# Moving three pieces of a fused attention and two-layer kernel: y products one tile earlier, the first units' stores to GpSimd's queue, and two pieces of the last product to an earlier pool

## The chip, the cores and the metric

The kernel runs on one core of a Trainium2 chip. The metric is device time in microseconds of one execution; each kernel is run several times and the median is given. TensorE (PE, with its weight loads PEld), VectorE (DVE), ScalarE (ACT), GpSimd (POOL) and SyncE (SP, which only issues DMAs here) each run their own instructions in the order in which they stand in the program.

## What is computed

The reference, cut to what matters:

```python
def _attn_ref(q, k, v):                      # (8, 8, 576, 64), chunks of 64
    scores = scale * q_c @ k_c.T
    attn = softmax(scores)
    return attn @ v_c
def _moe_ref(x, w_in, w_out, g_ln):          # 4608 tokens, 512 -> 1024 -> 512
    h = x @ w_in
    solu = h * softmax(h)
    ln = (solu - mean) / sqrt(var + 1e-06) * g_ln
    return ln @ w_out                        # "y" below
def _moe2_ref(x, w_in, w_out, alpha):        # 512 -> 2048 -> 512
    h = x @ w_in
    g = maximum(h, 0) + alpha * minimum(h, 0)
    return g @ w_out
reference = moe2(moe(attention(q, k, v)))
```

Every matrix product is made to float32 accuracy out of three products of a high and a low part (high by high, high by low, low by high).

## The kernel before, in words

**Phase 1** walks over 36 tiles of 128 tokens: attention, `h`, softmax and layer norm, transposed back (`zt`, `zh`, `zl`), then the y product of the tile. Its order is written out by hand: `FIRST` for the first ten tiles, then `STEP` (line 70) once for every tile i from 10 to 35, then `LAST` (line 81). An entry such as `ye-7` does the step `ye` of tile i-7; an entry that has been done already is passed over. `LAST` begins with `zh34 zl34 ya30 yb30 ye29 zt35 zh35 zl35 ye30 ya31`. `ya` and `yb` (`ymm`, line 567) are the two halves of one y product, `ye` (`yevac`, line 582) copies it out of PSUM on ScalarE and stores it. A y product s needs the tiles of its pair (s and s+1 for even s). The PSUM tile `yps` has one buffer; for `LAST` a second one is opened (line 654), and product s takes the one with number (s+1) mod 2. The `zh`/`zl` pairs have three buffers (line 177), the PSUM tile `zt` has one (line 182).

**Phase 2, first product.** The 4608 tokens are six groups s of 768 (each as two halves of 384 columns), the 2048 columns of the layer eight blocks b. Strassen's scheme makes a unit (`unit`, line 821) out of seven products `p1 p6 p5 p7 p2 p3 p4` in the PSUM tiles x, y, z, v, and four results `g` of it: "22", "11", "12", "21", in this order, in six buffers. Each is stored by a DMA `gd<-g` on SP (`store`, line 806). The results "12" and "21" are finished and stored inside the next unit (`late`, line 809). `load_y` (line 721) fetches the next group's y, `sum_y` (line 729) adds its parts on GpSimd; both are called from `extra` (line 1003), at places named (b, k). In the first group the weights of blocks 4 to 7 are also loaded by `extra`.

**Phase 2, second product.** It is cut into 40 pieces x = (chunk c, group g, block pair j), the first of them (0,0,0) to (0,0,3). A piece is loaded (`load_g`, line 897: a, b, c and, from the results "11", "12", "22", "21"), turned into operands (`prepare`, line 918: on DVE three operations for p1, three for p5, one each for p6 and p7, with copies on ScalarE) and multiplied (`multiply`, line 940). Piece (0,0,0) is loaded and prepared beside the last group's units, in the slots that group's y leaves free (`slot`, line 712: a list of 25), and its `t4` lies in a pool of its own (line 690). The others lie in the pool `rp` (line 1036), which is opened after the pool of these slots has been closed and takes over its memory: a load into it waits until what lay there has been read. SP takes eight DMAs in flight: each waits for the one eight places ahead of it on the DMA queues of SP and ScalarE.

Of the kernel before, what the change touches and what calls it, by code (L numbers as in the profile page):

```python
# [33 lines left out]
SG = 384  # L34
# [8 lines left out]
def order(text):  # L43
# [25 lines left out]
)  # L69
STEP = order(  # L70
    """
    q+3 v+3 ye-7 zh-2 zl-2 conv+0 hm+0 tr+1 te+1 qk+2 hx+0 he+0 qm+2 qe+2 pv+1 zt-1 xn+1 so+0 sq+0
    ya-6 conv+1 xt+1 xh+1 xl+1 zv+0 pw+0 qs+2 zs+0 yb-6
    """
)
CONV = order(
# [13 lines left out]
def tile_chunk_attention_solu_prelu(  # L90
# [30 lines left out]
    wo_dram = dram.tile([128, NB2, 2, 7, 256], F32, name="wod")  # L121

    g_dram = [dram.tile([128, NB2, PAIRS], F32, name=f"gd{i}") for i in range(4)]

    def fetch64(raw, src):

# [555 lines left out]
    def phase2():  # L682
        with ExitStack() as c2:
            def P(name, bufs, side="left", stack=c2, **k):
                return stack.enter_context(tc.tile_pool(name=name, bufs=bufs, side=side, reuse_waits="tile", **k))
# [1 line left out]
            NL = 2  # L687
            wl = P("w2l", 1)
            ps2 = [P("ps_2l", 1, space=PSUM)]
            kp = P("k4", 1)  # L690
            ca = c2.enter_context(ExitStack())
            tp = P("t2", 1, stack=ca)
            up = P("u2", 1, stack=ca)
# [12 lines left out]

            slots = [f"y{i}" for i in range(25)]
            homes = {}  # L710

            def slot(dtype, name):
# [36 lines left out]
            class Unit:  # L749
# [54 lines left out]
                    )  # L804

                def store(self, t):
                    nc.sync.dma_start(out=GD[t][:, self.b, self.s * SG:self.s * SG + SG], in_=self.g[t])

                def late(self, k):

# [76 lines left out]

            def new(x, tag, dtype=F32R):
                n = CHUNKS[x[0]][1]
                if x == (0, 0, 0):  # L890
                    if tag == "t4":
                        return kp.tile([128, 2, n], dtype, name="t4", tag="t4")
                    return slot(dtype, f"f{tag}")[:, :, :n]
                bufs = dict(t3=1, t2=1, t4=4, hi=4, lo=3).get(tag, 2)
                return rp.tile([128, 2, 512], dtype, name=f"r{tag}", tag=tag, bufs=bufs)[:, :, :n]

            def load_g(x):
                c, g, j = x
                p0, n = CHUNKS[c]
                for tag, t in (("a", "11"), ("b", "12"), ("c", "22"), ("d", "21"))[2 * g:]:  # L900
                    src[x, tag] = new(x, tag, F32 if tag == "b" else F32R)
                    nc.sync.dma_start(
                        out=src[x, tag].bitcast(F32), in_=GD[t][:, 2 * j:2 * j + 2, p0:p0 + n]
                    )

            def split(x, p, f, out):
                h = new(x, "hi")
# [10 lines left out]
            def prepare(x, p):  # L918
                a, b, c, d = (src.get((x, t)) for t in "abcd")
                k = x[0], x[2]  # L920
                if p == "p1":
                    low_ = split(x, p, a, a)
                    t3 = src[x, "t3"] = new(x, "t3", F32)
                    dsub(t3, c, b)
                    dsub(b, b, a)
                    low_()
                elif p == "p5":
                    low_ = split(x, p, b, None)
                    t2 = src[x, "t2"] = new(x, "t2", F32)
                    dsub(t2, c, b)  # L930
                    t4 = t4s[k] = new(x, "t4", F32)
                    dsub(t4, d, t2)
                    low_()
                else:
                    f = dict(p6=src.get((x, "t2")), p7=src.get((x, "t3")), p2=d, p3=c, p4=t4s.get(k))[p]
                    split(x, p, f, f if p in ("p2", "p3") else None)()

            bank, acc, out_ = {}, {}, []

# [61 lines left out]
            for s in range(NS):  # L1001
                for b in range(NB2):
                    def extra(k):
                        if s == 0 and k == 1 and NL + 2 + b < NB2:
                            load_w(NL + 2 + b, wi_dram)
                        if s + 1 == NS:
                            x = (0, 0, 0)
                            if (b, k) == (0, 3):
                                load_g(x)
                            if k == 2 and 4 <= b:  # L1010
                                prepare(x, GROUPS[0][b - 4])
                        else:
                            if (b, k) == (0, 3):
                                load_y(s + 1)
                            if (b, k) in sums:
                                sum_y(sums[b, k])
                            if (b, k) in early:
                                high_y(s + 1, early[b, k])
                            if (b, k - 1) in early:
                                low_y(s + 1, early[b, k - 1])  # L1020
# [8 lines left out]
                        load_w(b, wo_dram)  # L1029
            for k in range(3):  # L1030
                prev.late(k)
            for t in range(4):
                multiply(t)
            ca.close()

            rp = P("g3", 2)
            op = P("o3", 1)
            LEAD = 3
            load_g(pieces[1])
            load_w(6, wo_dram)  # L1040
            load_g(pieces[2])
            load_w(7, wo_dram)
            for t in range(4, 4 + LEAD):
                prepare(steps[t][:3], steps[t][3])
            for t in range(4, len(steps)):
                for n, x in enumerate(pieces[3:], 3):
                    if start[pieces[n - 2]] + 2 == t:
                        load_g(x)
                if t + LEAD < len(steps):
                    prepare(steps[t + LEAD][:3], steps[t + LEAD][3])  # L1050
                multiply(t)
                evacuate(t)
# [36 lines left out]
```

## Time and profile before

| | |
|---|---|
| median of 3 runs | 1329.59 us (1328.49 to 1331.25) |
| the profiled execution | 1325.93 us |
| its span in the profile | 1324.1 us |
| PE busy | 1266.7 us, 96% |
| DVE, ACT, POOL busy | 946.5, 689.6, 328.9 us |
| granted clock, mean | 0.987 |

The profile is one execution; times in it count from the start of its span. Phase 1 ends and phase 2 begins at about 599 us, the second product begins at about 967 us. A busy PE says that matmuls were in it, and the granted clock (PEclk, 1.00 is full speed) how fast they could go.

### The profile page before, as it was taken

To read this page: it belongs to the slowest core of one execution; us is meant where nothing else is said; L and a number is where in the kernel's file an instruction comes from. 1 tells how busy PE (TensorE), PEld (TensorE's weight loads), DVE (VectorE), ACT (ScalarE), POOL (GpSimd) and SP (SyncE) were. 2 spreads that over 40 slices of the span, in tenths; PEclk is the share of its full clock that TensorE was granted. 3 is DMA by queue.
4 is the path that set the end of the run, shared out by engine and by line. 5 is a ranking of instruction groups with operands and counts; after the bars stand their busy time and mean duration, and the time that the engine had idled before them with its cause. 6 is when DMAs were issued, how large, how long until landed. Compare 5 with 4: busy or idle time off the path is not lost. (4 is left out here: it accounts for less than half of the span.)

```text
span 1324.1 us, 21433 instructions
## 1 busy us (share of the span) xinstructions
PE 1266.7 (96%) x7968; PEld 1167.5 (88%) x7968; DVE 946.5 (71%) x1425; ACT 689.6 (52%) x1140; POOL 328.9 (25%) x309
## 2 busy tenths in 40 slices
PE   4989989999999999998999999999989999999998
PEld 3778879999899989997999999999989888888898
DVE  6996676777767677424777777777766968868584
ACT  4685455555655654433656666666544444444443
POOL 4664254444645554222020202110000000000000
PEclk9799999999999999999999999999989999999999
DMA  9774267565757563348542433436985827465462
GB/s 232 173 169 117 82 164 176 147 172 167 216 163 215 169 190 128 106 170 340 207 156 102 161 123 136 149 114 234 323 313 156 281 85 272 140 232 197 135 231 96
DMA packets 214792, 236.30 MB, mean 178 GB/s; under 512 B 89248, under 2 KB 174240, under 8 KB 212640
## 3 DMA queue, kind: packets, MB, share of 16 engines
q1 hardware_dynamic: 204896, 225.49, 54.4%
q10 hardware_dynamic: 9792, 9.44, 2.1%
q8 instruction: 63, 1.03, 0.3%
q14 instruction: 41, 0.34, 0.1%
HBM read 148.90 MB, written 85.98 MB: 177 GB/s over the span
## 5 line engine op out<-in xcount | busy, mean ns | idle before, releaser
L802 DVE SCALAR_TENSOR_TENSOR g<-ng,nal,g 128x384 f32<-128x384 f32 x192 | 123.3, 642 | 62.2 <-ACT g L680 62.2
L160 PE MATMUL yps<-zh,wo_h 128*128 128x256 f32 x576 | 167.2, 290 | 0.0
L162 PE MATMUL yps<-zh,wo_l 128*128 128x256 f32 x576 | 163.0, 283 | 0.0
L161 PE MATMUL yps<-zl,wo_h 128*128 128x256 f32 x576 | 162.8, 283 | 0.0
L680 ACT ACTIVATE ng<-g 128x384 f32<-128x384 f32 x144 | 75.7, 526 | 140.4 <-DVE g L674 140.4
L763 PE MATMUL hx<-th,w 128*128 128x384 f32 x384 | 113.8, 337 | 5.0 <-ACT s L680 5.0
L763 PE MATMUL hv<-th,w 128*128 128x384 f32 x384 | 114.1, 337 | 4.2 <-DVE g L674 3.9
L763 PE MATMUL hz<-th,w 128*128 128x384 f32 x384 | 114.0, 337 | 2.9 <-DVE wv L674 2.9
L161 PEld LDWEIGHTS yps<-zl,wo_h 128*128 128x128 f32 x576 | 110.4, 192 | 0.1
L160 PEld LDWEIGHTS yps<-zh,wo_h 128*128 128x128 f32 x576 | 110.4, 192 | 0.1
L162 PEld LDWEIGHTS yps<-zh,wo_l 128*128 128x128 f32 x576 | 110.2, 191 | 0.0
L950 PE MATMUL oz<-rhi,w 128*128 128x512 f32 (+1 forms) x312 | 96.7, 371 | 1.2 <-DVE osb L674 1.2
L950 PE MATMUL ox<-rhi,w 128*128 128x512 f32 (+1 forms) x312 | 97.2, 373 | 0.0
L950 PE MATMUL ov<-rhi,w 128*128 128x512 f32 (+1 forms) x312 | 95.9, 368 | 0.0
L677 POOL TENSOR_TENSOR yt<-y,y 128x384 f32<-128x384 f32 x24 | 29.1, 1232 | 246.3 <-DMA y<-yd 197.2
L680 ACT ACTIVATE rhi<-rt 128x1024 fp32r<-128x1024 f32 (+1 forms) x57 | 55.5, 982 | 61.2 <-DVE rt L677 18.4
L481 PE MATMUL h<-wi_h,xh 128*128 128x512 f32 x256 | 71.0, 399 | 7.8 <-ACT xh L467 5.2
L763 PEld LDWEIGHTS hv<-th,w 128*128 128x128 f32 x384 | 71.3, 189 | 6.6 <-DVE g L674 4.9
L680 ACT ACTIVATE g<-g 128x384 f32<-128x384 f32 x144 | 75.2, 522 | 3.1
L763 PEld LDWEIGHTS hx<-th,w 128*128 128x128 f32 x384 | 71.3, 189 | 5.3 <-ACT s L680 5.3
L561 DVE TENSOR_TENSOR zl<-zt,zh 128x1024 fp32r<-128x1024 f32 x36 | 44.0, 1222 | 44.0 <-ACT zh L556 44.0
L763 PEld LDWEIGHTS hz<-th,w 128*128 128x128 f32 x384 | 71.3, 189 | 4.3 <-ACT th L680 4.3
(188 smaller groups left out, 3340.8 us busy)
## 6 DMA issues: line engine op xcount, KB each, us to landing
gd<-g SPq DMA_DIRECT2D x192, 192.0 KB, 1.9
w<-wid SPq DMA_DIRECT2D x8, 1792.0 KB, 10.6
w<-wod SPq DMA_DIRECT2D x8, 1792.0 KB, 9.7
rc<-gd SPq DMA_DIRECT2D x24, 512.0 KB, 4.0
rd<-gd SPq DMA_DIRECT2D x24, 512.0 KB, 4.9
raw<-in_moe_w_out SPq DMA_DIRECT2D x24, 511.8 KB, 4.2
qt<-in_q SPq DMA_DIRECT2D x36, 256.0 KB, 5.1
kbd<-in_k SPq DMA_DIRECT2D x72, 128.0 KB, 5.1
```

Of the source, the lines that this page charges most:

```text
L160: nc.tensor.matmul(o, lh, rh, start=first, stop=False)
L161: nc.tensor.matmul(o, lh, rl, start=False, stop=False)
L162: nc.tensor.matmul(o, ll, rh, start=False, stop=last)
L481: nc.tensor.matmul(ps[:, n], xh[:, kk], w[:, kk, 512 * n:512 * n + 512], start=(kk == 0 and w is wi_h), stop=False,)
L561: nc.vector.tensor_tensor(out=zl, in0=ps, in1=zh.bitcast(F32), op=ALU.subtract)
L677: eng.tensor_tensor(out=out, in0=a, in1=b, op=ALU.subtract)
L680: nc.scalar.activation(out=out, in_=in_, func=func, **k)
L763: nc.tensor.matmul(self.ps[x], w[:, a, i, k], d[:, k], start=(p not in CHAINED and k + j == 0), stop=(k == 1 and j == 2), skip_group_check ...
L802: nc.vector.scalar_tensor_tensor(out=self.g[t], in0=self.n[t], scalar=nal_sb[:, f:f + 1], in1=self.g[t], op0=ALU.mult, op1=ALU.add)
L950: nc.tensor.matmul(bank[key, m][:, :n], W[2 * j + k][:, a, i, 128 * m:128 * m + 128], d[:, k], start=(p not in CHAINED and j + k + q == 0) ...
```

## The change

The y products stand one tile nearer in `STEP`. In the first group all 32 stores of `g` go to GpSimd's DMA queue. Pieces (0,0,0) and (0,0,1) both lie in the y slots (one more of these, no `k4` pool); a slot is given back as soon as its last reader has been recorded; their `t4` is written to DRAM by GpSimd and read back for the second half of the chunk. Piece (0,0,1) is loaded at place (7,1) of the last group, prepared after its last unit and multiplied next. The last step of piece (0,0,0) is prepared at (7,0) rather than (7,2). The pieces after it are loaded one later, and weights 6 ahead of piece (0,0,2).

```diff
-    q+3 v+3 ye-7 zh-2 zl-2 conv+0 hm+0 tr+1 te+1 qk+2 hx+0 he+0 qm+2 qe+2 pv+1 zt-1 xn+1 so+0 sq+0
-    ya-6 conv+1 xt+1 xh+1 xl+1 zv+0 pw+0 qs+2 zs+0 yb-6
+    q+3 v+3 ye-6 zh-2 zl-2 conv+0 hm+0 tr+1 te+1 qk+2 hx+0 he+0 qm+2 qe+2 pv+1 zt-1 xn+1 so+0 sq+0
+    ya-5 conv+1 xt+1 xh+1 xl+1 zv+0 pw+0 qs+2 zs+0 yb-5
...
+    t4_dram = [dram.tile([128, 2, CHUNKS[0][1]], F32, name=f"t4d{i}") for i in range(2)]
...
-            kp = P("k4", 1)
-            slots = [f"y{i}" for i in range(25)]
+            slots = [f"y{i}" for i in range(26)]
...
                 def store(self, t):
-                    nc.sync.dma_start(out=GD[t][:, self.b, self.s * SG:self.s * SG + SG], in_=self.g[t])
+                    eng = nc.gpsimd if self.s == 0 else nc.sync
+                    eng.dma_start(out=GD[t][:, self.b, self.s * SG:self.s * SG + SG], in_=self.g[t])
...
             def new(x, tag, dtype=F32R):
-                if x == (0, 0, 0):
-                    if tag == "t4":
-                        return kp.tile([128, 2, n], dtype, name="t4", tag="t4")
-                    return slot(dtype, f"f{tag}")[:, :, :n]
+                if x in pieces[:2]:
+                    return slot(dtype, f"f{tag}")
...
             def load_g(x):
+                if x in ((0, 1, 0), (0, 1, 1)):
+                    t4s[0, j] = new(x, "t4", F32)
+                    nc.sync.dma_start(out=t4s[0, j], in_=t4_dram[j])
...
             def prepare(x, p):
+                done = free if x in pieces[:2] else lambda t: None
                 if p == "p5":
...
+                    for t in (b, c, d):
+                        done(t)
+                    if x in pieces[:2]:
+                        nc.gpsimd.dma_start(out=t4_dram[x[2]], in_=t4)
+                        done(t4)
                 else:
...
+                    if p in ("p6", "p7"):
+                        done(f)
...
-                            x = (0, 0, 0)
                             if (b, k) == (0, 3):
-                                load_g(x)
-                            if k == 2 and 4 <= b:
-                                prepare(x, GROUPS[0][b - 4])
+                                load_g(pieces[0])
+                            if (b, k) == (7, 1):
+                                load_g(pieces[1])
+                            if (b, k) in ((4, 2), (5, 2), (6, 2), (7, 0)):
+                                prepare(pieces[0], GROUPS[0][b - 4])
...
-            for t in range(4):
+            load_w(6, wo_dram)
+            for p in GROUPS[0]:
+                prepare(pieces[1], p)
+            for t in range(8):
                 multiply(t)
             ca.close()
...
-            load_g(pieces[1])
-            load_w(6, wo_dram)
             load_g(pieces[2])
             load_w(7, wo_dram)
-            for t in range(4, 4 + LEAD):
+            load_g(pieces[3])
+            for t in range(8, 8 + LEAD):
                 prepare(steps[t][:3], steps[t][3])
-            for t in range(4, len(steps)):
-                for n, x in enumerate(pieces[3:], 3):
+            for t in range(8, len(steps)):
+                for n, x in enumerate(pieces[4:], 4):
```

**GpSimd at the start of phase 2** (`gd<-g` is a store of a result, `yt<-y` and `y<-y` are the sums of the next group's y). Before:

```order
L873 TENSOR_SCALAR nal<-al_sb 128x16
L677 TENSOR_TENSOR yt_6846<-y_6793,y_6791 128x384 x2
L677 TENSOR_TENSOR y_6791<-y_6791,y_6789 128x384 x2
L677 TENSOR_TENSOR yt_7013<-y_6793,y_6791 128x384 x2
L677 TENSOR_TENSOR yt_7097<-y_6795,yt_7013 128x384 x2
```

and with the change:

```order
L875 TENSOR_SCALAR nal<-al_sb 128x16
L809 DMA gd_76<-g 128x384
L809 DMA gd_73<-g 128x384
L679 TENSOR_TENSOR yt_6845<-y_6792,y_6790 128x384 x2
L809 DMA gd_74<-g 128x384
L809 DMA gd_75<-g 128x384
L809 DMA gd_76<-g 128x384
L809 DMA gd_73<-g 128x384
L679 TENSOR_TENSOR y_6790<-y_6790,y_6788 128x384 x2
L809 DMA gd_74<-g 128x384
L809 DMA gd_75<-g 128x384
```

The first two stores ("22" and "11" of the first unit) stand ahead of the first sum; "12" and "21" of the first unit and "22" and "11" of the second stand behind it.

**ScalarE at the end of phase 1** (`zh<-zt` are the copies of tiles 33 to 35, `ysb<-yps` the copies of y products). Before:

```order
L556 ACTIVATE zh<-zt 128x8x128
L586 ACTIVATE ysb<-yps 128x512
L588 DMA yd_69<-ysb 128x2x256
L556 ACTIVATE zh<-zt 128x8x128
L586 ACTIVATE ysb<-yps 128x512
L588 DMA yd_70<-ysb 128x2x256
L586 ACTIVATE ysb<-yps 128x512
```

and with the change:

```order
L558 ACTIVATE zh<-zt 128x8x128
L238 ACTIVATE hi<-s_6130 128x512
L238 ACTIVATE hi<-s_6131 128x512
L503 ACTIVATE eh,st<-h,st 128x1024
L519 ACTIVATE eh,st<-sl,st 128x1024
L558 ACTIVATE zh<-zt 128x8x128 x2
L588 ACTIVATE ysb<-yps 128x512
L590 DMA yd_70<-ysb 128x2x256
L588 ACTIVATE ysb<-yps 128x512
```

The y product 29 has been copied out inside `STEP`, and the copies of tiles 34 and 35 now follow each other; the first copy behind them is that of y product 30.

**SP at the end of the last group**, with the engines that each DMA waits for (`gd<-g` are the last unit's stores, `w<-wod` weights 6 and 7, `fa` to `fd` the piece in the y slots, `ra` to `rd` pieces in the pool `rp`). Before:

```order
L807 DMA gd_76<-g 128x384 [waits DMAHW0_49,DVE_49]
L807 DMA gd_73<-g 128x384 [waits DMAHW1_49,DVE_49]
L807 DMA gd_74<-g 128x384 [waits DMAHW2_49,DVE_49]
L807 DMA gd_75<-g 128x384 [waits DMAHW3_49,DVE_49]
L902 DMA ra<-gd_73 128x2x384 [waits DMAHW4_49,PE_49]
L902 DMA rb<-gd_74 128x2x384 [waits PE_49,DMAHW5_49,Activation_49,Pool_49]
L902 DMA rc<-gd_76 128x2x384 [waits DMAHW6_49,PE_49,Activation_49]
L902 DMA rd<-gd_75 128x2x384 [waits DMAHW7_49,PE_49]
L705 DMA w_10883<-wod 128x3584 [waits DMAHW0_49]
L902 DMA ra<-gd_73 128x2x384 [waits DMAHW1_49]
L902 DMA rb<-gd_74 128x2x384 [waits DMAHW2_49]
L902 DMA rc<-gd_76 128x2x384 [waits DMAHW3_49]
```

and with the change:

```order
L902 DMA fc<-gd_76 128x2x384 [waits DMAHW2_49,DMASW4_49,Activation_49]
L902 DMA fd<-gd_75 128x2x384 [waits DMASW7_49,DMAHW3_49,DMASW3_49,PE_49]
L809 DMA gd_76<-g 128x384 [waits DMAHW4_49,DVE_49]
L809 DMA gd_73<-g 128x384 [waits DMAHW5_49,DVE_49]
L809 DMA gd_74<-g 128x384 [waits DMAHW6_49,DVE_49]
L809 DMA gd_75<-g 128x384 [waits DMAHW7_49,DVE_49]
L706 DMA w_10818<-wod 128x3584 [waits DMAHW0_49]
L902 DMA ra<-gd_73 128x2x384 [waits DMASW5_49,DMASW1_49,DMAHW1_49,DVE_49,PE_49]
L902 DMA rb<-gd_74 128x2x384 [waits DMASW6_49,DMASW2_49,DMAHW2_49,PE_49,Pool_49]
L902 DMA rc<-gd_76 128x2x384 [waits DMAHW3_49,DMASW4_49]
L902 DMA rd<-gd_75 128x2x384 [waits DMAHW4_49,DMASW7_49,DMASW3_49]
L706 DMA w_10964<-wod 128x3584 [waits DMAHW5_49]
```

The piece behind the one in the slots is now loaded ahead of the last unit's stores, into slots (`fa` to `fd`), and the first `ra` to `rd` are the third piece's; weights 6 stand ahead of them. The second of these four loads, `rb`, has a wait for PE. By the count in the built program this is the last matmul with the low part of p6 of the piece before, (0,0,1), the third of its four products.

## Rows read from the trace of the kernel before

**Rows 1.** The page, busy time of each engine

```profile
PE 1266.7 (96%) x7968; PEld 1167.5 (88%) x7968; DVE 946.5 (71%) x1425; ACT 689.6 (52%) x1140; POOL 328.9 (25%) x309
```

**Rows 2.** Windows: length, busy PE, PEld, DVE, ACT, POOL (count); PEclk; DMA; GB/s

```profile
180.00:190.00 10.00, 4.78 (x23) 3.96 (x23) 7.94 (x16) 6.25 (x11) 2.52 (x4) 0.84 0.84 190
...
620.00:630.00 10.00, 5.11 (x16) 5.11 (x17) 6.42 (x11) 4.43 (x10) 7.83 (x8) 0.68 1.05 397
...
980.00:990.00 10.00, 10.00 (x44) 10.00 (x45) 7.94 (x10) 3.27 (x4) 0.00 (x0) 0.73 1.01 396
```

**Rows 3.** Timeline, PE, h of tile 11: start, us, line, count [idle before <-releaser]

```profile
186.91 2.08 PE L481 MATMUL h<-wi_h,xh 128*128 128x512 f32 x4 [5.22 <-ACT xh L467]
188.79 1.71 PE L481 MATMUL h<-wi_l,xh 128*128 128x512 f32 x4
190.33 1.08 PE L481 MATMUL h<-wi_h,xh 128*128 128x512 f32 x4
```

**Rows 4.** Windows, the matmuls of y alone, two products (29 and 30)

```profile
558.10:569.90 11.80, 11.75 (x96) 11.58 (x96) 0.60 (x1) 1.00 1.01 374
```

**Rows 5.** Timelines of PE, DVE and ACT, end of phase 1

```profile
569.75 1.04 PE L543 MATMUL zt<-ident,sl 128*128 128x128 f32 x8
...
564.11 1.50 DVE L532 TENSOR_SCALAR sl<-sl,st 128x1024 f32<-128x1024 f32 x1 [0.66 <-POOL st L528]
565.53 1.21 DVE L561 TENSOR_TENSOR zl<-zt,zh 128x1024 fp32r<-128x1024 f32 x1
...
570.82 1.03 ACT L556 ACTIVATE zh<-zt 128x1024 fp32r<-128x1024 f32 x1 [5.12 <-PE zt L543]
571.74 0.60 ACT L586 ACTIVATE ysb<-yps 128x512 f32<-128x512 f32 x1
```

**Rows 6.** Timelines of PE, DVE and POOL, start of phase 2

```profile
624.89 0.69 PE L763 MATMUL hx<-th,w 128*128 128x384 f32 x1 [5.02 <-ACT s L680]
...
621.91 0.56 DVE L674 TENSOR_TENSOR g<-hz,u 128x384 f32<-128x384 f32 x1 [5.80 <-DMA gd<-g]
...
626.55 0.56 DVE L674 TENSOR_TENSOR g<-hv,wv 128x384 f32<-128x384 f32 x1
...
619.17 1.96 POOL L677 TENSOR_TENSOR yt<-y,y 128x384 f32<-128x384 f32 x2 [46.62 <-DMA y<-yd]
```

**Rows 7.** DMA issues: count, KB, us to landing; the last at 600.25

```profile
gd<-g SPq DMA_DIRECT2D x192, 192.0 KB, 1.9
...
yd<-ysb ACTq DMA_DIRECT2D x36, 256.0 KB, 2.1
...
yd<-ysb ACTq DMA_DIRECT2D x1, 256.0 KB, 13.4
```

**Rows 8.** Chain that ended last: start, us, what (first, third piece)

```profile
967.23 2.08 PE ox L950 x12
...
990.75 2.08 PE ox L950 x12
```

**Rows 9.** Timelines of PE and DVE, start of the second piece

```profile
979.74 0.69 PE L950 MATMUL ox<-ra,w 128*128 128x384 f32 x1 [3.85 <-DVE ra L677]
...
976.67 0.96 DVE L677 TENSOR_TENSOR rt<-rc,rb 128x768 f32<-128x768 f32 x1 [6.23 <-DMA rc<-gd]
```

**Rows 10.** Timelines of ACT and DVE in the last unit

```profile
962.84 0.84 ACT L680 ACTIVATE fhi<-ft 128x768 fp32r<-128x768 f32 x1
...
962.56 0.56 DVE L674 TENSOR_TENSOR u<-hy,s 128x384 f32<-128x384 f32 x1 [0.20 <-ACT s L680]
...
963.56 0.55 DVE L674 TENSOR_TENSOR wv<-hz,u 128x384 f32<-128x384 f32 x1
964.03 0.95 DVE L677 TENSOR_TENSOR flo<-ft,fhi 128x768 fp32r<-128x768 f32 x1
```

**Rows 11.** DMA issues from 969.9 to 972.6: count, KB, us to landing

```profile
ra<-gd SPq DMA_DIRECT2D x1, 384.0 KB, 3.6
rb<-gd SPq DMA_DIRECT2D x1, 384.0 KB, 4.1
```

## The prediction

> **What bounds the kernel now.** I read the busy times first: TensorE has matmuls in it for 96% of the span [rows 1], so only its idle time can be won, and time in which its clock is low. The windows show where that is: three stretches of ten us have little work or a granted clock of 0.84, 0.68 and 0.73 [rows 2]. 1.00 is the 2.4 GHz level; a mean below it mixes 2.4 and 1.2 GHz. The change touches all three, so I went to the timeline of each. In the first, TensorE idles 5.22 before the h product of tile 11, for which ScalarE's copy is late; the product then starts slowly, 2.08 and 1.71 for four matmuls that take 1.08 at full speed, so 1.6 is lost [rows 3]. In the second, at the start of phase 2, VectorE waits 5.80 for a store of `g` to land, and TensorE 5.02 [rows 6]. In the third, TensorE idles 3.85 before the second piece of the last product, whose load VectorE waited 6.23 for [rows 9]. Each time the clock fell behind idle time of 3.85 or more. The cost of a fall is 1.6 (counted matmul by matmul), 2.7 and 3.2 (27% and 32% of ten us, a little of it in idle time) [rows 2, 3]. I use these three as the price of a fall.
>
> **The y products.** Two y products take 11.75, one 5.9 [rows 4]. *At the beginning*: step 10 had no y product, because its entry was done already. Now it has one, in the place where TensorE idled. The h product of tile 11 starts at 181.7 + 5.9 = 187.6 instead of 186.9, at full speed: -1.6 + 0.7 = -0.9. From there each step holds the next y product in the same place, and its inputs are two tiles old or more, so nothing changes until the end. *At the end*: one y product less stands between the last h product and the transpose of tile 35, so TensorE reaches that at 569.75 - 5.9 = 563.9. But the transpose's PSUM tile is free only when VectorE has made the low part of tile 34, which stands behind the scaling of tile 35 and ends at 565.53 + 1.21 = 566.7 [rows 5]. This chain hangs on the last h product and doesn't move: TensorE idles 2.9. Then y product 31 has to use the PSUM tile of product 30 (now made while there was only one), and the copy that frees it stands behind tile 35's on ScalarE. In these rows that copy ends 571.74 + 0.60 - 569.75 = 2.6 after the transpose began, so there are 1.6 more idle behind a transpose of 1.0 [rows 5]. Against a product of 5.9 stand 4.5 idle: -1.4. Together -2.3. The idle 2.9 and 1.6 have only a transpose between them, and I expect the clock to fall there: its price is 1.6 to 3.2, I take 2.4. **Sum of this part: +0.1, ends -2.3 and +0.9.**
>
> **The stores.** Today the first unit's stores stand on SP behind weights and y. In GpSimd's queue the first two ("22", "11") can go at once, and the second unit's wait of 5.80 goes. What is late next: "12" and "21" stand behind the first `sum_y`, and GpSimd waits in that until the y loads have landed; it begins at 619.17 and takes 1.96 [rows 6]. VectorE needs the buffer of "12" for the third unit's first result. Queued behind the waiting GpSimd are these two stores and the second unit's; VectorE, then TensorE, wait for them. So "12" goes at 621.1, when weights 5 to 7 fill the DMA engines: 3 x 1792 KB, at the 397 GB/s of that stretch [rows 2] some 14 us, until about 634. No row shows a store of GpSimd's queue. The low end is a store as on the page, 1.9 [rows 7]: landed at 623.0, and the third unit's first result comes 3.5 before today's 626.55 [rows 6]. The high end is the one store that another queue made beside such loads: ScalarE's of y took 13.4 instead of 2.1 [rows 7]. It has two rows of 1 KB per partition, a `g` store has one; half of the extra 11.3 makes 5.6, so 7.5 to landing and 5.6 for each one behind it. Then "12" lands at 628.6, 2.1 later than today's result, and the third store behind the sums at about 636, where today's third result of that unit is 3 behind its first, at 629.5. Of these 6.5 late the next unit's first products, on the other PSUM tiles, cover about 2: +4.5. The first row is of an idle moment and the second of ScalarE's queue; neither is nearer, so I take the middle: **+0.5, ends -3.5 and +4.5.** TensorE idles some 4 or more there either way, so the clock falls as it does today and its price is in both.
>
> The Trainium skill (DMA: Bandwidth & Descriptors, section Issuing engines are not separate DMA queues) speaks against this part: DMAs of all issuing engines run on the same 16 DMA engines and interleave, and another issuing engine only saves the time to issue. The row of ScalarE's store, 13.4 beside the loads, agrees with it; by that rule the sum would be nearer the high end.
>
> GpSimd's own time for 32 stores, and for two stores of `t4`, lies beside an engine that is 25% busy [rows 1]; were it over 1.5 a store it would hold up the next sums, which have three units of slack. The two `t4` stores and loads are 384 KB each, against some 3.6 for such a load alone [rows 11], and are due tens of us later: nothing.
>
> **The pieces.** Piece (0,0,1) is loaded before the last unit's stores and is multiplied right behind the first: the idle 3.85 goes. Against this stand two things. *The last step of piece (0,0,0)* is prepared earlier in the last unit, and VectorE then waits in it for ScalarE's copy `fhi`, which ends at 962.84 + 0.84 = 963.7; with its 0.95 behind that, `u` starts at 964.6 instead of 962.56, and `wv` ends at 966.1 instead of 964.1 [rows 10]. Product p3 needs that; it began two products of 1.04 before the first piece, at 965.1 [rows 8]. So the first piece starts 1.0 later, at 968.2. *The third piece's load*: the load of b waits for p6 of the second piece, because its memory held that operand, and c stands behind b. Eight products of 2.08 [rows 8] end at 984.9, the third of the second piece's four at 982.8. b is issued then and c half a us later; first and second of a row of loads take 3.6 and 4.1 [rows 11], so c lands at 987.4. From VectorE's first operation on it to TensorE's start there are 979.74 - 976.67 = 3.1 [rows 9]: the third piece starts at 990.5. It starts at 990.75 now [rows 8]. So the stall isn't removed but moved by one piece, to 5.6 of idle time, and -0.2 is left. The slow stretch behind today's stall is inside the 990.75; the new one comes after the 990.5. It costs again 1.6 to 3.2, I take 2.7, the row of the stall it replaces. **+2.5, ends +1.4 and +3.0.** Weights 6 and 7 and the fourth piece land some 8 us ahead of their use; the work behind is the same.
>
> **Sum:** 0.1 + 0.5 + 2.5 = +3.1. The profiled execution took 1325.93, so 1329.0 for such a one; the median of the runs is 1329.59, 3.7 above it, and with the same difference I get 1332.7. The ends together make -4.4 and +8.4.
>
> **Rivals.**
> *GpSimd's queue is slow* (the high end): the third and fourth unit wait for stores behind the sum. For it: the 13.4 row, and a GpSimd that waits to 621. Against: the store has half the rows. 0.1 + 4.5 + 2.5 = +7.1: 1336.7. This is also the case in which that part doesn't do what it says.
> *GpSimd's queue is quick*: its stores land in about 1.9 beside the loads. 0.1 - 3.5 + 2.5 = -0.9: 1328.7. The Trainium skill (the same page, section Queues, rings and completion order) says that a DMA engine changes between queues by whole packets of several descriptors; by that rule a store would get through in few turns and the time would be this one. No row here shows a packet of GpSimd's.
> *Faster, the third piece's load isn't held*: if b is issued by about 976.5, c lands by 981, and the third piece starts right at 984.9, 5.8 before today's 990.75, without a fall of the clock. 0.1 + 0.5 - 5.8 = -5.2: 1324.4. For it: the loads stand ahead of other work by then, and the DMA engines are idle. Against: b's wait stands in the order of SP, and c is in the same queue behind it. It decides at the wait of the first `rb`.
>
> **How the numbers follow.** 0.40 for the forecast, 0.25 for the slow queue, 0.20 for the quick one, 0.15 for the load that isn't held. 0.2% is 2.7 us, about what a measurement of this kernel can tell from no change. The slow queue is slower, the quick one no change, the third faster; the forecast lies at the edge, a little over half of it slower. That makes slower 0.48, same 0.33, faster 0.19. The range takes in the quick and the slow case with their ends and leaves out the third: 1326.5 to 1337.5; the forecast's own range is 1330.5 to 1335.
>
> **What would show it.** No idle time before h of tile 11; 2.9 and 1.6 idle around the transpose of tile 35, and a granted clock below 1.00 behind it; TensorE waiting in the third unit instead of the second, before its last product, for a store of GpSimd's; no idle time before the second piece, some 5.6 before the third, with the first `rb` issued when p6 of the second piece ends. I am wrong if the clock stays up at the end of phase 1 (-2.4), if stores of GpSimd's queue land in 2 us, or if the third piece starts without a wait.

## The result and the profile after

The changed kernel takes 1337.24 us (median of 8 runs, 1332.92 to 1339.54) against 1328.78 for the one before on the same chip (8 runs, 1326.41 to 1331.25): a ratio of 1.006, 95% interval 1.0045 to 1.0075. It is slower, by about 8.5 (6.0 to 10.0). The forecast was 1332.7, slower by 3.1. The time lies outside the forecast's own range (1330.5 to 1335), 0.3 inside the wide one (to 1337.5), and beside the rival of the slow GpSimd queue, which gave 1336.7.

The profiled execution took 1335.51, its span 1333.7. Busy time answers to [rows 1]:

```profile
PE 1269.7 (95%) x7968; PEld 1168.9 (88%) x7968; DVE 948.2 (71%) x1425; ACT 689.7 (52%) x1140; POOL 344.6 (26%) x343
```

The engines have the work that they had, but for GpSimd's 34 DMA instructions (its busy time is 15.7 more); 9.6 of span were added, of which TensorE's matmuls fill 3.0. To see where, I took the start of the same matmul in both timelines of TensorE (the start of the second product and of the third piece from the chain of waits) and let each stretch show what it added:

| stretch, by TensorE | before | after | added | forecast |
|---|---|---|---|---|
| start to h of tile 10 | 171.55 | 173.63 | +2.1 | 0 |
| to h of tile 12 | 203.53 | 204.37 | -1.2 | -0.9 |
| to the first product of phase 2 | 599.42 | 601.22 | +1.0 | +1.0 |
| to the third unit of the second group | 682.73 | 691.00 | +6.5 | +0.5 |
| to the last unit but one | 952.50 | 960.66 | -0.1 | 0 |
| to the second product | 967.23 | 976.72 | +1.3 | +1.0 |
| to the third piece | 990.75 | 998.82 | -1.4 | -1.2 |
| to the end of the span | 1324.1 | 1333.7 | +1.5 | +2.7 |

The first stretch is the same in both programs; in the other kernels below it took 0.3 to 4.4 more than in the profile of before, which happens to be an early one. It isn't the change's. The rest, 7.5, agrees with the runs, and one stretch holds nearly all of it: the start of phase 2.

The windows of after (columns as in [rows 2]):

```profile
180.00:190.00 10.00, 10.00 (x91) 9.74 (x90) 7.97 (x14) 4.58 (x8) 3.66 (x4) 1.00 0.95 216
560.00:570.00 10.00, 6.44 (x51) 6.00 (x50) 4.73 (x9) 4.52 (x7) 5.03 (x6) 0.95 1.02 380
570.00:580.00 10.00, 10.00 (x64) 10.00 (x64) 0.36 (x1) 1.18 (x2) 3.55 (x5) 0.71 0.49 200
620.00:630.00 10.00, 4.41 (x26) 4.08 (x24) 2.19 (x5) 1.37 (x4) 6.96 (x10) 0.85 1.04 423
630.00:640.00 10.00, 7.70 (x30) 7.39 (x30) 3.58 (x6) 3.62 (x8) 2.90 (x5) 0.64 0.86 355
990.00:1000.00 10.00, 4.71 (x25) 4.39 (x24) 4.08 (x5) 2.02 (x3) 0.00 (x0) 0.78 0.87 311
```

The window of tile 11 is full now and at full clock. At 560 to 580 there is a stretch of idle time and lower clock that wasn't there. At 620 to 640 two windows are bad where in [rows 2] one was: 12.1 busy of 20 where it was 15.1, at clocks of 0.85 and 0.64.

**Start of phase 2.** Timelines of TensorE, VectorE and GpSimd; they answer to [rows 6]:

```profile
632.30 0.69 PE L764 MATMUL hv<-th,w 128*128 128x384 f32 x1 [7.90 <-DVE g L676]
...
631.69 0.56 DVE L676 TENSOR_TENSOR g<-hv,wv 128x384 f32<-128x384 f32 x1 [9.14 <-DMA gd<-g]
...
636.33 0.56 DVE L676 TENSOR_TENSOR g<-hz,u 128x384 f32<-128x384 f32 x1 [2.32 <-DMA gd<-g]
...
608.30 0.76 POOL L809 DMA_DIRECT2D gd<-g  x1 [34.75 <-DVE g L803]
609.30 0.55 POOL L809 DMA_DIRECT2D gd<-g  x1 [0.24 <-issue]
623.02 1.97 POOL L679 TENSOR_TENSOR yt<-y,y 128x384 f32<-128x384 f32 x2 [13.18 <-DMA y<-yd]
624.93 2.15 POOL L809 DMA_DIRECT2D gd<-g  x4
```

GpSimd sends the first two stores at 608.3 and 609.3 and then stands 13.18 before the first sum, whose y has to land. Four stores, of the first and the second unit, wait behind it and go at 624.9 to 626.6. VectorE waits 9.14 for the first of them to land, since it needs that buffer, and TensorE waits 7.90 for VectorE. The DMA issues tell why they are slow as well (the last number of a row is the median time from issue to landing); first those from 608 to 617 and from 624.5 to 627 of after:

```profile
w<-wid SPq DMA_DIRECT2D x3, 1792.0 KB, 19.5
gd<-g POOLq DMA_DIRECT2D x2, 192.0 KB, 8.4
...
gd<-g POOLq DMA_DIRECT2D x4, 192.0 KB, 9.2
```

and those from 616 to 635 of before, about the same place in the program:

```profile
w<-wid SPq DMA_DIRECT2D x3, 1792.0 KB, 9.5
gd<-g SPq DMA_DIRECT2D x9, 192.0 KB, 5.0
```

Weights 5 to 7 went out at 616.9, 626.4 and 634.5 before, one after each unit's stores. Now no store stands ahead of them on SP, so they go at 608.7, 616.1 and 616.5 and take 19.5 (median of the three) where they took 9.5, side by side with the stores, which take 9.2 where SP's took 5.0. The two windows from 620 to 640 move 423 and 355 GB/s, at DMA shares of 1.04 and 0.86: the DMA engines are full in the first and nearly so in the second.

**End of phase 1 and second product.** TensorE, then the chain and SP and VectorE around the third piece (they answer to [rows 5, 8, 9]):

```profile
566.95 1.09 PE L545 MATMUL zt<-ident,sl 128*128 128x128 f32 x8 [1.96 <-DVE zl L563]
569.64 0.58 PE L162 MATMUL yps<-zh,wo_h 128*128 128x256 f32 x1 [1.60 <-ACT ysb L588]
...
998.82 0.69 PE L961 MATMUL ox<-ra,w 128*128 128x384 f32 x1 [5.29 <-DVE ra L679]
```

```profile
976.72 2.08 PE ox L961 x12
...
998.82 3.82 PE ox L961 x11
```

```profile
988.65 0.37 SPq L902 DMA_DIRECT2D ra<-gd  x1
991.18 0.37 SPq L902 DMA_DIRECT2D rb<-gd  x1
...
995.69 0.96 DVE L679 TENSOR_TENSOR rt<-rc,rb 128x768 f32<-128x768 f32 x1 [7.11 <-DMA rc<-gd]
```

The two waits at tile 35 are there (2.9 and 1.6 were forecast), the third piece waits 5.29 (5.6 was), and `rb` goes 2.5 behind `ra`, when p6 of the second piece has been read. One matmul of the last unit waits 1.02, as forecast.

### The profile page after: what moved, and what is told of

Read it like the earlier page. It is cut to its first block, busy times and chain, and to the rows that moved or that the text cites. A ratio compares the mean times of both kernels' runs of the same rounds, so it can differ in the third digit from the quotient of the medians.

```text
span 1333.7 us, 21442 instructions
## 1 busy us (share of the span) xinstructions
PE 1269.7 (95%) x7968; PEld 1168.9 (88%) x7968; DVE 948.2 (71%) x1425; ACT 689.7 (52%) x1140; POOL 344.6 (26%) x343
## 5 line engine op out<-in xcount | busy, mean ns | idle before, releaser
L764 PE MATMUL hv<-th,w 128*128 128x384 f32 x384 | 114.6, 339 | 12.7 <-DVE g L676 12.5
L961 PE MATMUL oz<-rhi,w 128*128 128x512 f32 (+1 forms) x304 | 93.8, 369 | 0.8 <-DVE osb L676 0.8
L764 PEld LDWEIGHTS hv<-th,w 128*128 128x128 f32 x384 | 71.2, 189 | 15.7 <-DVE g L676 13.7
L679 DVE TENSOR_TENSOR rlo<-rt,rhi 128x1024 fp32r<-128x1024 f32 (+1 forms) x56 | 62.4, 1124 | 15.8 <-ACT rhi L682 15.5
```

Of the source, the lines that this page charges most:

```text
L679: eng.tensor_tensor(out=out, in0=a, in1=b, op=ALU.subtract)
L764: nc.tensor.matmul(self.ps[x], w[:, a, i, k], d[:, k], start=(p not in CHAINED and k + j == 0), stop=(k == 1 and j == 2), skip_group_check ...
L961: nc.tensor.matmul(bank[key, m][:, :n], W[2 * j + k][:, a, i, 128 * m:128 * m + 128], d[:, k], start=(p not in CHAINED and j + k + q == 0) ...
```

## Experiments

Times are medians of all runs beside the runs of the kernel before on the same chip. Where a stage is compared I use two lengths in the profiles that don't hold the first tiles: from h of tile 10 to the end (1152.6 before, 1160.1 after) and, for the stores, from the first product of phase 2 to the third unit of the second group (83.3 and 89.8).

### Each part alone

**The y products alone**: the change of `STEP` in the kernel before.

> The y products one tile nearer, the rest as before. Theory (from the positions in the two traces): -1.2 at tile 11, +1.0 at the end of phase 1, so no difference that can be measured: 1328.6 against a median of 1328.8, with idle time of about 2.0 and 1.6 around the transpose of tile 35 and a slow clock behind it, and none before h of tile 11. The prediction had +0.1. Rival: the whole loss of 8.5 needs the y products (the slow stretch at the end of phase 1 is what delays phase 2): then 1331 or more, and the same long wait at 624.

1326.59 (12 runs), ratio 0.9981 (0.9967 to 0.9995). From h of tile 10 to the end it is 1.7 shorter.

```profile
565.62 1.09 PE L543 MATMUL zt<-ident,sl 128*128 128x128 f32 x8 [1.97 <-DVE zl L561]
568.31 0.58 PE L160 MATMUL yps<-zh,wo_h 128*128 128x256 f32 x1 [1.60 <-ACT ysb L586]
```

The same waits, and this part is a small gain, not a loss: -1.2 to tile 12, then -0.4 to phase 2 where the whole change had +1.0. A y product of 5.9 [rows 4] less, 3.6 idle more: the clock's fall cost 2.0 here and 3.3 in the other execution, behind the same idle time.

**The stores alone**:

```diff
-                    nc.sync.dma_start(out=GD[t][...], in_=self.g[t])
+                    eng = nc.gpsimd if self.s == 0 else nc.sync
+                    eng.dma_start(out=GD[t][...], in_=self.g[t])
```

> Only the first group's stores in GpSimd's queue. Theory: this part is nearly all of the loss, +6.4, so 1335.2; VectorE waits some 9 in the third unit for the first store behind the first sum, TensorE some 8. The prediction had +0.5, so 1329.3, with an end at +4.5, so 1333.3. Rival: the stores cost that much only with the other parts in place (phase 2 begins with other transfers in flight): then 1331 or less.

1335.01 (11 runs), ratio 1.0051 (1.0031 to 1.0071). TensorE and VectorE wait as in the whole change:

```profile
632.62 0.69 PE L763 MATMUL hv<-th,w 128*128 128x384 f32 x1 [8.04 <-DVE g L674]
...
632.00 0.56 DVE L674 TENSOR_TENSOR g<-hv,wv 128x384 f32<-128x384 f32 x1 [9.29 <-DMA gd<-g]
```

The first product of phase 2 to the third unit of the second group takes 89.9, 6.6 more than before. This part is nearly the whole loss, and needs neither of the others.

**The pieces alone**: the rest of the change.

> Only the second piece in the slots, with what belongs to it. Theory: +1.2 by the positions in the two traces, so 1330.0: no idle time before the second piece, 5.3 before the third, one slow stretch of the clock, and about 1.0 lost in the last unit. The prediction had +2.5, so 1331.3, for the same events. Rival: the stall of the third piece grows where the stores of the first group are on SP's queue, since SP then comes later to the loads: 1332 or more.

1331.81 (12 runs), ratio 1.0021 (1.0006 to 1.0036), 2.8 by the runs and 2.3 from h of tile 10 to the end. The two waits are those of the forecast, 1.0 and 5.6:

```profile
969.10 0.44 PE L764 MATMUL hz<-th,w 128*128 128x384 f32 x1 [1.02 <-DVE wv L676]
993.55 0.69 PE L960 MATMUL ox<-ra,w 128*128 128x384 f32 x1 [5.26 <-DVE ra L679]
```

By the ratios, the three parts add up: -2.5 + 6.8 + 2.8 = +7.1, against 8.5 (6.0 to 10.0) for the whole.

### Why the stores cost so much

Two reasons are mixed in the trace: the stores go late, behind the sum; and they land late, beside weights that are no longer held back. The first can be taken away by itself, the second less cleanly: weights that are held back must stand in some queue.

**The sums behind the second unit's stores**, on top of the stores alone:

```diff
+            late_sums = {(2, 2): 0, (3, 2): 1, (4, 2): 2, (5, 2): 3}
-                            if (b, k) in sums:
-                                sum_y(sums[b, k])
+                            if (b, k) in (late_sums if s == 0 else sums):
+                                sum_y((late_sums if s == 0 else sums)[b, k])
```

> The stores in GpSimd's queue as in the run with these alone, but the four sums of the second group's y stand later in that queue, the first of them behind all stores of the first two units. Theory A, the stores are late because they stand behind a sum that waits for the y loads: nothing of the first unit's stores is issued later than 613, VectorE doesn't wait for the first of them, and the loss goes but for 1 to 2: 1328 to 1331. Theory B, they are late because weights 5 to 7, no longer held back by stores on SP, are issued together and fill the DMA engines: the stores issued after 616 still take 8 to 12, the wait comes for the second unit's stores instead, and 4 or more of the loss stays: 1333 or more.

1329.23 (12 runs), ratio 0.9993 (0.9976 to 1.0011): theory A by the time. But its trace shows that B is true as well, two units later. TensorE, and the DMA issues from 621 to 633:

```profile
619.16 0.44 PE L763 MATMUL hv<-th,w 128*128 128x384 f32 x1 [1.90 <-DVE g L674]
640.32 0.44 PE L763 MATMUL hx<-th,w 128*128 128x384 f32 x1 [1.10 <-ACT s L680]
...
645.54 0.64 PE L763 MATMUL hv<-th,w 128*128 128x384 f32 x1 [2.33 <-DVE g L674]
```

```profile
gd<-g POOLq DMA_DIRECT2D x8, 192.0 KB, 8.7
```

No store waits behind the sum, and TensorE has no long wait until 640: the start of the fourth unit comes 7.2 earlier than before, counted from the first product of phase 2. Then stores that took 8.7 beside the weights make it wait in the fifth unit, the clock falls, and 6.1 of the 7.2 are gone by the start of the seventh unit. So with the sum out of the way the loss is gone, though the weights still run beside the stores: the first product of phase 2 to the third unit of the second group takes 82.2, 1.1 less than before and 7.7 less than with the stores alone.

**The weights held back alone**: on top of the stores alone, weights 5 to 7 issued by GpSimd (a third argument of `load_w`) at the places where SP issued them, behind the stores of the unit before; the sums where the change has them.

> The sums where the change has them, only the three weights behind the stores in GpSimd's queue. Theory: the store behind the first sum still goes at about 623 to 624, but finds the DMA engines less full and lands in 2 to 4 instead of 6.6; TensorE waits about 4 to 5 in the third unit, as long as before, not 8: about 1329. Rival, the sum alone decides: it waits 7 or more, 1334.

One execution, 1336.20: from h of tile 10 to the end 5.6 more than before, from the first product of phase 2 to the third unit of the second group 89.4, 0.6 less than with the stores alone. So the rival is nearer by the time, though the first wait is that of the theory: the two stores behind the sum now land in 2.2 and 2.4, and TensorE waits 3.43 in the third unit. But the next two stand behind weights 5 in GpSimd's own queue and take 8.4, and TensorE waits again. So this run doesn't show what the weights alone are worth.

```profile
631.22 0.44 PE L763 MATMUL hv<-th,w 128*128 128x384 f32 x1 [3.43 <-DVE g L674]
640.98 0.69 PE L763 MATMUL hx<-th,w 128*128 128x384 f32 x1 [4.26 <-ACT s L680]
```

**Both, with weights 5 to 7 in GpSimd's queue**:

> As the run with the sums behind the stores, and weights 5 to 7 of the first group in GpSimd's queue too, behind the stores of the unit before, so that they are held back again as they were by the stores on SP. Theory, both reasons are true and the waits of the fourth to sixth unit in the last run come from these weights: no idle time over 2 between 620 and 660 and no slow clock, so the whole stage ends some 7 earlier than before: 1321 to 1323. Rival: the DMA engines are simply full until 640 whoever issues, and a store or a weight is late in any order: a wait of 3 or more stays, 1326 to 1329.

1329.4 (11 runs), ratio 1.0001 (0.9989 to 1.0013): a miss. TensorE waits 4.48 at 642, a wait of the size that the rival had, but the order makes it: the sums were blocked again, later.

```profile
634.83 1.99 POOL L677 TENSOR_TENSOR yt<-y,y 128x384 f32<-128x384 f32 x2 [10.98 <-DMA y<-yd]
```

```profile
y<-yd SPq DMA_DIRECT2D x4, 384.0 KB, 28.5
```

Weights 5, and then 6, ran in GpSimd's queue beside the y loads of SP's queue, which took 28.5 instead of the 20.0 of the run with the sums behind; the sum began at 634.8 and held the stores of the third unit. On SP these weights stood in line behind y. So each of them has its own time: y by the first sum, weights 6 and 7 only by the seventh and eighth unit.

**Stores mended**: sums as above, weights 5 on SP as in the change, weights 6 and 7 in GpSimd's queue, one unit later in the program than on SP.

```diff
-                        if s == 0 and k == 1 and NL + 2 + b < NB2:
-                            load_w(NL + 2 + b, wi_dram)
+                        if s == 0 and k == 1 and b in (0, 1, 3, 4):
+                            load_w((4, 5, 0, 6, 7)[b], wi_dram, nc.gpsimd if b > 1 else nc.sync)
```

> The stores alone, mended as in the run with the y products, which are where they were before: the sums behind the second unit's stores, weights 6 and 7 in GpSimd's queue behind the stores of the third and fourth unit. It differs from the run with the sums behind in these two weights alone. Theory: they were what took back the gain there, so the waits at 640 to 646 go: from the first product of phase 2 to unit 10 it takes 3 less than before, as with the y products, and the whole 1324 to 1326. Rival: with the y products in their old place phase 2 begins with other transfers in flight, and the gain seen beside them came from that: 1328 or more, as with the sums behind alone.

1323.28 (5 runs), ratio 0.9953 (0.9939 to 0.9966). The first product of phase 2 to the third unit of the second group takes 78.5, 4.8 less than before. The theory holds, and the gain is a little above it (4.8 where it had 3, 1323.3 where it had 1324 to 1326): with the stores, the sums and these two weights in an order by need, the queue that cost 6.8 gains 5.9. In the windows of this kernel nothing of [rows 2]'s second stretch is left:

```profile
620.00:630.00 10.00, 10.00 (x59) 10.00 (x59) 7.78 (x13) 6.34 (x14) 5.13 (x8) 1.00 1.04 410
630.00:640.00 10.00, 10.00 (x60) 10.00 (x59) 7.96 (x14) 6.14 (x13) 5.74 (x10) 1.00 0.91 352
```

### The waits at the end of phase 1

**Its order written anew**, with the y products one tile nearer:

```diff
-    zh34 zl34 ya30 yb30 ye29 zt35 zh35 zl35 ye30 ya31 yb31 sy0 ye31 ya32 yb32 sy1 sy2 ye32 ya33 yb33 sy3 sy4
+    zh34 zl34 ye30 ya31 yb31 zt35 zh35 zl35 sy0 ye31 ya32 yb32 sy1 sy2 ye32 ya33 yb33 sy3 sy4
...
-                    ypend[s] = ypools[(s + 1) % len(ypools)].tile(...)
+                    ypend[s] = ypools[s % len(ypools)].tile(...)
```

> The y products one tile nearer, and the last part of phase 1 written out anew: the copy of y product 30 ahead of that of tile 35 on ScalarE, y product 31 ahead of the transpose of tile 35 and in the second PSUM tile. Theory, the two idle times at the end come from this order alone: both go, and the slow clock with them. With 5.2 idle and 1.6 slow gone at tile 11 and nothing in their place, 1328.3 - 6.8 = 1321.5. Rival: the transpose of tile 35 or the next y products wait as long for something else (the high and low part of tile 35): 1325 or more.

1320.64 (5 runs), ratio 0.9939 (0.9921 to 0.9958), 8.2 less. From h of tile 10 to the first product of phase 2 it takes 420.9 instead of 427.9, 7.0 less, which is the 6.8 of the theory; the rest lies behind that. Both waits are gone, and the clock stays at full speed:

```profile
555.00:565.00 10.00, 10.00 (x72) 9.32 (x71) 4.37 (x8) 4.37 (x8) 2.81 (x3) 1.00 0.74 253
565.00:575.00 10.00, 10.00 (x86) 10.00 (x86) 3.26 (x4) 3.51 (x6) 8.61 (x10) 1.00 1.02 423
```

The y products cover tile 11's wait, and the work that was missing at the end for that is there again: the move gains what the wait cost only if the end doesn't pay it back.

### The third piece's wait

**Other slots for the operands of the first two pieces**, so that the memory which the third piece's a to d take over holds no operand of the second piece's products; the first piece is multiplied before the second is prepared, and its operands' slots are given back then; weights 6 stand behind the third piece's loads. The main lines of it:

```diff
-                    return slot(dtype, f"f{tag}")
+                    return slot(dtype, f"f{tag}", late_ if x == pieces[1] and tag in ("hi", "lo") else early_)
...
...
-            load_w(6, wo_dram)
...
             load_g(pieces[2])
+            load_w(6, wo_dram)
             load_w(7, wo_dram)
```

> The pieces alone, with other slots for the operands of the first two pieces, so that the memory of the third piece's a to d is free when the last unit ends, weights 6 behind these loads, and the slots of the first piece given back as its products are recorded. Theory, the third piece's wait comes from the memory its load of b takes over: b is issued by 981 and not at 991, the 5.3 idle and the slow stretch behind it go, and nothing else is late: 1331.8 - 7.0 = 1324.8. Rival: the wait moves on to the fourth piece, whose loads now stand behind weights 6 and 7: 4 or more idle there, 1330 or more.

1329.89 (11 runs), ratio 1.0009 (0.9999 to 1.0019), against 1.0021 for the pieces as they are. `rb` now goes half a us behind `ra`, before the second piece is multiplied, and the third piece starts without a wait. The rival is right all the same: the wait moves on, the fourth piece waits 0.65 and 3.81. SP, the fourth piece's wait on TensorE, and the issues from 973.5 to 983, each `ra` and `rb` row there for the third and the fourth piece together:

```profile
973.77 0.45 SPq L904 DMA_DIRECT2D ra<-gd  x1
974.32 0.53 SPq L904 DMA_DIRECT2D rb<-gd  x1
...
1000.06 0.60 PE L963 MATMUL ox<-ra,w 128*128 128x384 f32 x1 [3.81 <-DVE ra L679]
```

```profile
w<-wod SPq DMA_DIRECT2D x2, 1792.0 KB, 10.4
ra<-gd SPq DMA_DIRECT2D x2, 384.0 KB, 9.4
rb<-gd SPq DMA_DIRECT2D x2, 384.0 KB, 10.1
```

The fourth piece's loads stand behind 3.6 MB of weights and take 14.3 to 15.5.

**Weights 6 ahead of the last unit's stores** (with the reordered y products):

> The reordered y products with the pieces as in the run with the third piece free, and weights 6 loaded right behind the second piece's loads, ahead of the last unit's stores, instead of behind the third piece's. Theory: the fourth piece waited because 3.6 MB of weights lay ahead of its loads; with half of them moved into the last unit, where the DMA engines were 70% busy, its loads land some 4 earlier and 4.5 of idle time with the slow stretch behind it shrink to 1 or less: 1320.6 + 1.1 - 6 = 1316. Rival: the weights only push back the loads of the second and third piece, and a wait of 3 or more stands before one of these: 1320 or more.

1319.88 (6 runs), ratio 0.9937 (0.9923 to 0.9951), no better than the y products alone with 0.9939. The fourth piece no longer waits, but the third does again, for its load, and the clock falls:

```profile
983.91 0.69 PE L963 MATMUL ox<-ra,w 128*128 128x384 f32 x1 [2.68 <-DVE ra L679]
```

In the four orders the wait stood before the second, the third, the fourth and again the third piece. In this last one the DMA engines were busy all the time from 965 to 985 (shares of 1.02 and 1.04 in the two windows), so I read it as a matter of how much has to land there; that no order removes it isn't shown.

### Together

**Reordered y products and mended stores**:

> The reordered y products (1320.6 alone) with the stores in GpSimd's queue, the sums behind the stores of the second unit, weights 5 on SP as before, and weights 6 and 7 in GpSimd's queue behind the stores of the third and fourth unit, some 8 later than SP issued them in the run with the sums behind. Theory: there the gain of 7 at the third unit was lost again because these two weights, needed 8 to 10 after they landed, ran beside stores that were needed at once; held back, they leave the stores 3 to 5, and most of the 7 stays: 1314 to 1316. Rival: weights, y and stores together fill the DMA engines up to 640 in any order, and something is late again: 1319 to 1321.

1315.77 (6 runs), ratio 0.9913 (0.9897 to 0.9928), as the theory had it: 12.5 less than before, where the y products alone gave 8.2.

**All three parts mended**:

> The last two together: every part of the change, each mended. If they add up as the parts of the change did: 1320.6 - 6 - 5 = 1310 where both theories hold, 1315 where one does, 1321 where none does.

1316.17 (5 runs), ratio 0.9914 (0.9899 to 0.9929): the case in which one of the two theories holds, that of the stores. It can't be told apart from the kernel without the pieces. From h of tile 10 to the end the two profiles are 11.0 (without the pieces) and 13.7 less than before. Either beats both kernels; the simpler one, without the pieces, is the one to keep.

## Why the prediction was right and wrong

**The y products** (+0.1, ends -2.3 and +0.9). This part was right in its events and nearly in its sum: -0.9 at tile 11 was -1.2; of the idle 2.9 and 1.6, the first was 1.96, because the low part of tile 34 came 0.6 sooner and the y product ended 0.3 later than worked out. In the whole change the part gave -0.2, alone -1.7. What the forecast took as the price of the fall, 2.4, was 3.3 and 2.0. It said nothing of what the experiment shows: that the loss at the end came from the order there and could be had back.

**The stores** (+0.5, ends -3.5 and +4.5) is the step that failed. It was +6.5, beyond the high end. What was wrong in it:

- *The middle between the ends.* "The first row is of an idle moment and the second of ScalarE's queue; neither is nearer, so I take the middle." The second was nearer. The forecast itself put the store at a time when weights fill the DMA engines. Of such a time were the 13.4 of ScalarE's store and SP's own stores there, with SP's loads ahead of them in line: 15.4 for the one sent at 606 and a median of 5.0 for nine later ones; the 1.9 was the median over 192 stores, most of them in quiet stretches. The four stores behind the sum took 6.6, 8.2, 10.2 and 12.0; 7.5 was the forecast's high end for the first.
- *The sum of the high end.* By its own 5.6 for each store behind the first, the third would have landed at 628.6 + 11.2 = 639.8 and not at "about 636", which makes a high end of +8.3 and a middle of +2.4. It landed at 636.23, or 634.4 without the 1.8 by which phase 2 began later: the written 636 was near it, but not by the stated working.
- *The start of the sum.* It was taken from before, 619.17 or 621.0 with the 1.8 by which phase 2 began later. It began at 623.02. The weights 4 ahead of y in SP's queue took 16.3 instead of 15.3, beside the first two stores in GpSimd's queue, and the third y load, for which the sum waits, took 19.0 instead of 17.0. Of these two us one comes with the weights; where the other comes from isn't shown. Weights 5 aren't it: they stand behind y in the same queue, and from 619 to 621.9 all but 12 of the 735 packets are under 2 KB, as y's are.

The fall of the clock wasn't the error: the forecast had its price the same in both, and in the stretch from the first product of phase 2 to the third unit of the second group TensorE's idle time rose from 6.9 to 12.5, by 5.6, and the time in matmuls from 76.4 to 77.2, by 0.9.

One thing the forecast didn't ask: what the stores on SP had held back. With them gone from that queue, weights 6 and 7 went 10 and 18 sooner and ran beside the stores. Of the loss itself, though, the place of the sum is nearly all: with the sums moved behind the stores, and the weights as they are, 5.8 of 6.8 come back by the medians and 7.7 by the length of that stretch. With weights 5 to 7 held back and the sums left in place 0.6 of 6.6 do, but in one execution, and with these weights ahead of stores in GpSimd's own queue. What the weights decide is whether the move gains: with the sums behind the stores and weights 6 and 7 held back it ends 5.9 below the kernel before, where the stores alone ended 6.8 above it.

The Trainium skill's rule that DMAs of all issuing engines run on the same 16 DMA engines and interleave (DMA: Bandwidth & Descriptors, section Issuing engines are not separate DMA queues), which the forecast weighed against this part, is what the rows show: 9.2 per store beside the weights. The rival of the slow queue had the right mechanism, stores behind the sum for which the third unit waits, though the queue itself isn't slow: behind the same sum, with the weights held back, two of its stores landed in 2.2 and 2.4. The rival of the quick queue was wrong: beside the loads its stores took 6.6 to 12.0 and not 1.9.

**The pieces** (+2.5, ends +1.4 and +3.0): right. The last unit's wait was 1.02 (forecast 1.0), the third piece's 5.29 (5.6), `rb` went when p6 of the second piece had been read, and the third piece came 1.4 earlier against the start of the second product (1.2). Mis-sized was the fall's price: from the third piece to the end the whole change lost 1.5, not 2.7. Alone the part cost 2.8 by the runs. The rival of a load that isn't held would have been wrong even with the wait on p6 gone: its 5.8 were to be gained at the third piece, and in the run with the third piece free the wait moves on to the fourth.

**The sum.** +3.1 was forecast and +8.5 measured; the two parts that were right stand at -0.2 and +1.4 in the profile, and the third at +6.5. The forecast's chances don't follow from its cases either: with a little over half of the forecast slower, "same" would be 0.37 and "faster" 0.15, not 0.33 and 0.19.

## What to carry to other kernels

A DMA that waits for a result also holds back every DMA behind it in its queue. Before you move it to another queue, list what will go sooner then, when that is needed, and which transfer it will run beside. Take a transfer's price from the stretch in which it will run, not from a median over the kernel: where the DMA engines are full, what matters is who is first, and a load that is needed tens of us later must not go beside a store that a buffer waits for. Look also at what stands ahead in the new queue: here it was a sum that waited for loads. And when work is moved forward into a hole, follow the order to the place from which it was taken.

## What of the hardware was not expected

GpSimd's queue is about as quick as SP's in a quiet stretch: its 192 KB stores land in 2.1 (median of the 22 issued after 640 in the first group), SP's in 1.9 (median of all), and cost GpSimd 0.54 each, 17 for the 32 of the first group. A transfer shares the DMA engines with another queue's but stands in line in its own: the same y loads took 20.0 with weights 5 behind them on SP, and 28.5 with these weights, and then weights 6, in GpSimd's queue. And the fall of the clock has no fixed price: behind idle times of 1.96 and 1.60 at the same place it cost 3.3 in one execution and 2.0 in another; idle times of 1.9 alone, at the second unit, have no slow stretch behind them in any of these traces.
